# Attention, routed experts and a second MoE on one core: exponentials side by side for the product with V, and ids, gathers, low parts and flags in another order

## The chip, the core and the metric

The kernel runs on one core of a Trainium2 chip. The core has TensorE (PE: matmuls and transposes into PSUM), VectorE (DVE), ScalarE (ACT), GpSimd (POOL) and SyncE (SP, which issues most transfers), each with a queue of its own that it works through in order; the 16 DMA engines move data between HBM and SBUF. The metric is the device time of one launch in microseconds; lower is better.

## What is computed

```python
def _attn_ref(q, k, v, f):                    # B=4, H=8, S=576, D=64
    scores = np.matmul(q, k.transpose(0, 1, 3, 2)) / np.sqrt(D)
    cum = np.cumsum(np.log(np.clip(f, 0.0001, 1.0)), axis=-1)
    scores = scores + cum[:, :, :, None] - cum[:, :, None, :]
    scores = np.where(causal, -1000000000.0, scores)
    attn = np.exp(scores - np.max(scores, axis=-1, keepdims=True))
    attn = attn / (np.sum(attn, axis=-1, keepdims=True) + 1e-09)
    return np.matmul(attn, v)

def _moe_ref(x, modality_id, w_gate, modality_bias, w1, w2):   # N=2304, D=512, E=8, F=1024
    logits = x @ w_gate + modality_bias[modality_id]
    e_idx = np.argmax(logits, axis=1)
    gate_w = softmax(logits)[np.arange(N), e_idx]
    for e in range(E):
        mask = e_idx == e
        out[mask] = gate_w[mask, None] * (np.maximum(x[mask] @ w1[e], 0.0) @ w2[e])

def _moe2_ref(x, w1, w2, w3, w_out):          # d_ff=768
    return np.maximum(np.maximum(x @ w1, x @ w2), x @ w3) @ w_out
```

The rows of the attention's output, 4 x 576 tokens of 512, go through the routed experts and then through the second MoE.

## The kernel before

By the times of its trace the kernel has three stages: attention with the routing and one "early" expert to 303 us, the slots of the other experts to 505, and the second MoE to the end.

**Attention.** The 576 keys and queries of a head are cut into four blocks of 128 and a tail of 64 (index 4; `BLK` holds start and length). Scores stand transposed, keys on the partitions. The tails of four heads share one tile (`tail_scores`, exponentials in `p4`). The rest of a head is three parts of 512 columns (`PARTS`, L436): each lists pieces (key block, query blocks, first column, last column), gets its matmuls (`st_mm`: L424 for the fp16 main part, L426 for a second part of low bits, decay and maximum), one exponential on ScalarE (L461) into `pt`, and a mask of the diagonal blocks on GpSimd (`causal`, L432). "all", "13" and "23" name sets of query blocks in the layout of q, which stores them in the order 0, 2, 1, 3. `WHERE` (L439) says in which part and column the exponentials of a pair of blocks lie.

**The product with V.** `av` (L470) multiplies the exponentials with `vb`, 64 columns of V and a column of ones, in f32. The first four query blocks of a head go to a PSUM tile `avt` of 512 columns (L490), the tail's 64 columns to columns 384 to 448 of one of two accumulators, `accs[h % 2]` (L487), in five products of 64. `av_sb` copies both on ScalarE to `os` (L495 for the tail, L496 for the 512), `av_tr` transposes `os` back into columns 0 to 325 of the same accumulator (L503), and VectorE divides by the sum of the row into `xacc` (L511 to L513).

**The order.** Attention runs in steps, one for each part of each head, 24 a batch; a step is about 2 us in the middle of the attention. `at(step, function, priority)` puts work into a step's agenda (`run_step` works it off), and `later(step, f, n, priority)` runs f in its step and what f returns n steps later. A head's products with V follow its scores by `AVL` = 5 steps. The instructions of an engine then stand in the order in which they were issued. Of the work in the agenda these pieces matter here:
- `second_q` (L1103): at the start, the transposed q of the second four heads of batch 0 is copied from PSUM to `qs` (L257 on VectorE, L255 on ScalarE) and doubled into q's second half (`dup`, L281).
- the maxima: products `m` on PE (L334 to L337), reduced on VectorE (L328).
- `mod_tr` in step 14 and `bias` in step 16 (L1141, L1142): the modality ids of all tokens are converted (`mc`, L987 to L989), transposed on PE (`mt`, L991) and turned into the bias of the logits (L997 to L1005). The logits that the bias is added to are made for the first time at the end of batch 0.
- `plan_early` (L824): the early expert is chosen from the first two batches' routing, its 256 tokens are gathered from DRAM, where `xd` holds the attention's rows as fp16 high and low parts, by two gathers issued by GpSimd (`e_gather`, L778, in steps 84 and 90, `EPL` + 10 and + 16), and transposed by SP into `ev` (L779) three steps later. Its matmuls start at `e_h(0)` (L789).
- `x_cols(0, 6)` in step 97 (L953): of the last batch's rows the columns of six heads are split into a high part on ScalarE and a low part on GpSimd (L544), one instruction for the four blocks of 128 rows and one for the tail.
- after the last step `route` computes ranks with one-hots `oh` (L657) and small products (L663 to L667).

**The slots.** `slot(s)` (L1454) runs expert work for one or two tiles of 128 tokens: `hgroup` (L1411 to L1416) makes the hidden layer, `ytile` the output rows, which GpSimd scatters. `split_next(s, ...)` splits the next slot's weights inside `tc.If(flag)`, where the flag is read on each engine (L1437).

## Time and profile before

| | before |
|---|---|
| median of 3 runs, us | 794.81 (793.76 to 798.06) |
| profiled execution, us | 798.22, its span 796.4 |
| mean granted TensorE clock | 0.969 |
| PE busy, us | 738.0 (93%) |
| VectorE, ScalarE, GpSimd busy, us | 405.9, 287.5, 223.2 |
| matmuls, DMA packets | 5244, 147105 (98.01 MB) |

The profiled execution is at the upper end of the runs. Its span is the time from the first to the last instruction; 1.8 us lie around it. Times within the trace count from the start of the span. "Busy" says when an engine was at work, not whether anybody waited for it. An idle time before an instruction is given in brackets with what ended it.

### The profile page before, as it was taken

The page shows a single profiled execution, that of the slowest core. Times are in us where ns is not written, and L with a number is a line of the kernel's source. Part 1 is how long each engine was busy: PE and PEld are TensorE (multiplying, and loading weights), DVE is VectorE, ACT ScalarE, POOL GpSimd, SP SyncE. Part 2 cuts the span into 40 slices and gives each one's busy share as a digit, 9 for nine tenths or more (in the row PEclk, how much of TensorE's full clock was granted, in tenths as well). Part 3 has the DMA queues.
Part 4 walks back from the last instruction along what each step waited for, and adds up shares of the span by engine and source line. Part 5 has one row for each costly group of instructions (what it writes and reads, how often), then busy time and mean ns, then how long its engine had stood idle before and what let it go on. Part 6 is the DMA issues. An engine that isn't in the chain of part 4 may idle for free.

```text
span 796.4 us, 14004 instructions
## 1 busy us (share of the span) xinstructions
PE 738.0 (93%) x5244; PEld 451.0 (57%) x5244; DVE 405.9 (51%) x862; ACT 287.5 (36%) x494; POOL 223.2 (28%) x374
## 2 busy tenths in 40 slices
PE   6886999999996987899999998799999999999996
PEld 3564667667764755666666665344444444444483
DVE  7775766765773374786984487398011021011010
ACT  7462545553453124433652265144111111111121
POOL 5551254353485010341122111012211211211211
PEclk9898999999998799999999999899999999999998
...
GB/s 168 143 57 187 98 169 199 101 159 55 205 101 80 25 168 306 191 143 340 269 169 133 265 256 202 186 221 1 53 1 1 106 0 1 67 13 1 40 14 27
DMA packets 147105, 98.01 MB, mean 123 GB/s; under 512 B 110576, under 2 KB 127076, under 8 KB 147013
## 3 DMA queue, kind: packets, MB, share of 16 engines
...
q14 instruction: 37, 0.30, 0.1%
...
## 4 chain that ended last, share of the span: by engine, by line
PE 44%; DVE 5%; issue 3%; DMA 2%; ACT 0%; POOL 0%; POOLq 0%; SPq 0%; ACTq 0%; DVEq 0%
PE a L1555 7%; PE a L1556 7%; PE a L1557 7%; PE y L1425 3%; PE o L1581 3%; PE h L1412 3%; PE h L1411 3%; PE y L1424 3%; PE h L1413 3%; PE y L1423 3%; PE o L1580 3%; PE o L1579 3%; DMA x2d<-ysb,ids 2%; DVE dec L1197 1%; DVE dec L1198 1%
## 5 line engine op out<-in xcount | busy, mean ns | idle before, releaser
L1555 PE MATMUL a<-xt,mwh 128*128 128x512 f16 (+1 forms) x360 | 130.0, 361 | 4.5 <-DVEq L1523 4.5
L1556 PE MATMUL a<-xt,mwh 128*128 128x512 f16 (+1 forms) x360 | 130.0, 361 | 0.0
L1557 PE MATMUL a<-xt,mwl 128*128 128x512 f16 (+1 forms) x360 | 129.8, 361 | 0.0
L432 POOL TENSOR_SCALAR_AFFINE_SELECT pt<-pt 64x128 f32<-64x128 f32 (+1 forms) x192 | 73.3, 382 | 98.7 <-ACT pt L461 87.7
L1561 DVE TENSOR_TENSOR s<-a,s 128x512 f32<-128x512 f32 (+1 forms) x30 | 19.1, 637 | 157.9 <-PE a L1557 156.7
L490 PE MATMUL avt<-pt,vb 128*65 128x128 f32 (+2 forms) x384 | 91.4, 363 | 2.7 <-POOL pt L432 2.6
L1411 PE MATMUL h<-xt,wh 128*128 128x256 f16 (+1 forms) x320 | 81.3, 264 | 6.4 <-DMA xt<-xg 4.2
L461 ACT ACTIVATE pt<-t 128x512 f32<-128x512 f32 x96 | 57.1, 596 | 80.5 <-PE t L426 77.4
L1564 POOL TENSOR_TENSOR hl<-s,hh 128x512 f16<-128x512 f32 (+1 forms) x30 | 32.8, 1093 | 186.2 <-ACT hh L1563 186.2
L1412 PE MATMUL h<-xt,wh 128*128 128x256 f16 (+1 forms) x320 | 81.4, 264 | 0.0
L1413 PE MATMUL h<-xt,wl 128*128 128x256 f16 (+1 forms) x320 | 81.3, 264 | 0.0
L328 DVE TENSOR_REDUCE cm<-m 128x1 f32<-128x512 f32 (+4 forms) x136 | 66.7, 533 | 10.2 <-PE m L337 8.0
L1387 DVE SCALAR_TENSOR_TENSOR wl<-raw,wh 128x1024 f16<-128x1024 f32 x48 | 57.0, 1221 | 14.5 <-ACT wh L1386 13.7
...
L1563 ACT ACTIVATE hh<-s 128x512 f16<-128x512 f32 (+1 forms) x30 | 17.6, 587 | 114.5 <-DVE s L1562 114.4
L1555 PEld LDWEIGHTS <-mwh 128*128 128x128 f16 x360 | 35.5, 99 | 40.6 <-DVEq L1523 5.0
L1425 PE MATMUL y<-wh,hl 128*128 128x512 f16 x144 | 54.6, 379 | 2.5 <-DVE hl L1416 2.0
L1557 PEld LDWEIGHTS <-mwl 128*128 128x128 f16 x360 | 35.5, 99 | 35.5 <-issue 1.4
L1556 PEld LDWEIGHTS <-mwh 128*128 128x128 f16 x360 | 35.5, 99 | 35.3 <-issue 1.1
L1423 PE MATMUL y<-wh,hh 128*128 128x512 f16 x144 | 54.6, 379 | 1.0 <-ACT hh L1415 1.0
L1386 ACT ACTIVATE wh<-raw 128x1024 f16<-128x1024 f32 x48 | 48.8, 1050 | 17.9 <-DMA raw<-in_moe_w_dram 10.6
L1424 PE MATMUL y<-wl,hh 128*128 128x512 f16 x144 | 54.6, 379 | 0.0
(328 smaller groups left out, 1407.4 us busy)
## 6 DMA issues: line engine op xcount, KB each, us to landing
...
```

The lines of the kernel that those rows point to most:

```text
L328: nc.vector.tensor_reduce(out=out, in_=in_, axis=AX.X, op=ALU.max)
L432: nc.gpsimd.affine_select(out=o, in_=o, pattern=[[0, nb], [1, 2], [2, HP]], base=-r2, channel_multiplier=-2, compare_op=ALU.is_ge, fill=0.0)
L490: nc.tensor.matmul(o[:D1, o0:o0 + n], vb[:, jb, h, :], pt[:, w, c0:c0 + n], start=(jb == 0), stop=(jb == min(o0 // 128 // 2 + 2 * (o0 // 1 ...
L1411: nc.tensor.matmul(ph[:, k], w1_(WH, s, c, fb), xt[:, c, 0:w], start=(c == 0), stop=False)
L1412: nc.tensor.matmul(ph[:, k], w1_(WH, s, c, fb), xt[:, NC + c, 0:w], start=False, stop=False)
L1413: nc.tensor.matmul(ph[:, k], w1_(WL, s, c, fb), xt[:, c, 0:w], start=False, stop=(c == NC - 1))
L1423: nc.tensor.matmul(py, hh[:, c, rs], w2_(WH, s, c), start=(c == 0), stop=False)
L1424: nc.tensor.matmul(py, hh[:, c, rs], w2_(WL, s, c), start=False, stop=False)
L1425: nc.tensor.matmul(py, hl[:, c, rs], w2_(WH, s, c), start=False, stop=(c == NF - 1))
L1555: nc.tensor.matmul(ps[:, :n], mwh[i][:, c, fs], xt[:, c, :n], start=(c == 0), stop=False)
L1556: nc.tensor.matmul(ps[:, :n], mwh[i][:, c, fs], xt[:, NC + c, :n], start=False, stop=False)
L1557: nc.tensor.matmul(ps[:, :n], mwl[i][:, c, fs], xt[:, c, :n], start=False, stop=(c == NC - 1))
```

## The change

1. Scores: part 0 has its query blocks in natural order ("nat"); part 1 begins with (block 0, tail) and goes on with key block 1 against 1, 2, 3 and the tail; part 2 holds key block 3 against 3 and the tail, then key block 2 against 2, 3 and the tail. So the exponentials of a key block stand side by side, and `av` issues products of 128 (into columns 384 to 512 of the accumulator), 448, 448, 320, 192 and 64 columns for a head. The copies are of 128 and 448 columns, the masks of part 2 pick their two blocks out of 384 columns.
2. `second_q`: all four copies on VectorE, the doubling of each half right behind its two, first in its step.
3. The ids: steps 26 and 27 instead of 14 and 16.
4. Both gathers of the early expert in step 97, their transposes two steps later.
5. `x_cols(0, 6)` two steps later, its low part in four pieces of 128 x 384 and one of 64 x 384.
6. In a slot of one tile the next slot's split, with its flag, stands before the output rows.

```diff
--- before.py
+++ after.py
@@ -296,6 +296,8 @@
         def sub(v_, cs):
             if cs == "all":
                 return v_
+            if cs == "nat":
+                return v_.rearrange("p a (b x) -> p b a x", b=2)
             if cs == "23":
                 return v_[:, :, 128:256]
             if cs == "01":
@@ -426,16 +428,16 @@
                 nc.tensor.matmul(o, part2(r, "k", 97, h, jb), part2(r, "q", 97, h, ib), start=False, stop=True, skip_group_check=True)
 
 
-        def causal(x, nb):
+        def causal(x):
+            nb = x.shape[1]
             for r2 in range(2):
-                o = x[HP * r2:HP * r2 + HP].rearrange("p (b r j) -> p b r j", b=nb, j=HP)
+                o = x[HP * r2:HP * r2 + HP].rearrange("p b (r j) -> p b r j", j=HP)
                 nc.gpsimd.affine_select(out=o, in_=o, pattern=[[0, nb], [1, 2], [2, HP]], base=-r2, channel_multiplier=-2, compare_op=ALU.is_ge, fill=0.0)
 
 
-        PARTS = (((0, "all", 0, 512),),
-                 ((1, "13", 0, 256), (1, 2, 256, 384), (0, 4, 384, 448), (1, 4, 448, 512)),
-                 ((3, 3, 0, 128), (2, "23", 128, 384), (2, 4, 384, 448), (3, 4, 448, 512)))
-        WHERE = {(0, 0): (0, 0), (0, 2): (0, 128), (0, 1): (0, 256), (0, 3): (0, 384), (1, 1): (1, 0), (1, 3): (1, 128), (1, 2): (1, 256), (3, 3): (2, 0), (2, 2): (2, 128), (2, 3): (2, 256), (0, 4): (1, 384), (1, 4): (1, 448), (2, 4): (2, 384), (3, 4): (2, 448)}
+        PARTS = (((0, "nat", 0, 512),),
+                 ((0, 4, 0, 64), (1, 1, 64, 192), (1, "23", 192, 448), (1, 4, 448, 512)),
+                 ((3, 3, 0, 128), (3, 4, 128, 192), (2, "23", 192, 448), (2, 4, 448, 512)))
 
         def tail_scores(u):
             b, hh = divmod(u, 2)
@@ -459,47 +461,40 @@
                 r["pt", h] = pt_p.tile([P, 3, 512], F32, tag="pt", name="pt", bufs=PTB)
             pt = r["pt", h][:, w]
             nc.scalar.activation(out=pt, in_=t, func=AF.Exp, scale=SC)
-            return lambda: causal(pt[:, 0:256] if w == 2 else pt[:, 0:128], 2 if w == 2 else 1)
+            blocks = (pt[:, 0:128], pt[:, 64:192], pt[:, 0:384])[w].rearrange("p (b x) -> p b x", b=1 + w // 2)
+            return lambda: causal(blocks[:, :, 0:128])
 
 
         D1 = D + 1
         TC = 384
 
-        AVP = ((0, ((0, 0, 512, 0),)), (1, ((1, 0, 256, 256), (1, 256, 128, 128))), (2, ((2, 128, 128, 128), (2, 256, 128, 384))), (3, ((2, 0, 128, 384),)))
+        AVP = ((128, 448, 0), (576, 448, 0), (1216, 320, 128), (1024, 192, 256))
 
         def av(b, h, jbs):
             r = bt[b]
-            vb, pt, p4 = r["vb"], r["pt", h], r["tail", h // HU]
+            vb, pt, p4 = r["vb"], r["pt", h].rearrange("p w x -> p (w x)"), r["tail", h // HU]
             if jbs[0] == 0:
                 r["o", h] = ps_w.tile([P, 512], F32, tag="o", name="avt")
+                nc.tensor.matmul(accs[h % 2][:D1, TC:TC + P], vb[:, 0, h, :], pt[:, 0:P], start=True, stop=True)
             o = r["o", h]
-            ot = accs[h % 2][:D1, TC:TC + HP]
             hc = HP * (h % HU)
             for jb in jbs:
                 if jb == 4:
-                    for k_ in range(NB):
-                        rows = HP if k_ == 4 else P
-                        if k_ == 4:
-                            x = p4[:, hc:hc + HP]
-                        else:
-                            w, cc = WHERE[k_, 4]
-                            x = pt[:, w, cc:cc + HP]
-                        nc.tensor.matmul(ot, vb[:rows, k_, h, :], x, start=(k_ == 0), stop=(k_ == 4))
+                    nc.tensor.matmul(o[:D1, 384:448], vb[:HP, 4, h, :], p4[:, hc:hc + HP], start=False, stop=True, skip_group_check=True)
                     continue
-                for w, c0, n, o0 in AVP[jb][1]:
-                    nc.tensor.matmul(o[:D1, o0:o0 + n], vb[:, jb, h, :], pt[:, w, c0:c0 + n], start=(jb == 0), stop=(jb == min(o0 // 128 // 2 + 2 * (o0 // 128 % 2), 9) or jb == 3), skip_group_check=True)
+                c0, n, o0 = AVP[jb]
+                nc.tensor.matmul(o[:D1, o0:o0 + n], vb[:, jb, h, :], pt[:, c0:c0 + n], start=(jb == 0), stop=(jb > 0), skip_group_check=True)
 
         def av_sb(b, h):
             r = bt[b]
             r["os", h] = sm.tile([D1, 512 + HP], F32, tag="os", name="os")
-            nc.scalar.activation(out=r["os", h][:, 512:512 + HP], in_=accs[h % 2][:D1, TC:TC + HP], func=AF.Copy)
-            nc.scalar.activation(out=r["os", h][:, 0:512], in_=r["o", h][:D1, :], func=AF.Copy)
+            nc.scalar.activation(out=r["os", h][:, 0:P], in_=accs[h % 2][:D1, TC:TC + P], func=AF.Copy)
+            nc.scalar.activation(out=r["os", h][:, P:576], in_=r["o", h][:D1, 0:448], func=AF.Copy)
 
         def av_tr(b, h):
             x = bt[b]["os", h]
             for ib in range(NB):
-                n = BLK[ib][1]
-                c = (0, 256, 128, 384, 512)[ib]
+                c, n = BLK[ib]
                 nc.tensor.transpose(accs[h % 2][:n, 65 * ib:65 * ib + 65], x[:, c:c + n], identf[:D1, :D1])
 
         def av_out(b, h):
@@ -541,7 +536,9 @@
             for y, n, cs in ((r["xh", 0], P, slice(0, 4)), (r["xh", 2], HP, slice(4, 5))):
                 xr = r["x"][:n, cs].rearrange("p c h d -> p c (h d)")[:, :, d]
                 nc.scalar.activation(out=y[:, :, 0, d], in_=xr, func=AF.Copy)
-                lo.append(lambda y=y, xr=xr: eng.tensor_tensor(out=y[:, :, 1, d], in0=xr, in1=y[:, :, 0, d], op=ALU.subtract))
+                for c in range(0, cs.stop - cs.start, 1 if hn > 2 else 4):
+                    c_ = slice(c, min(c + (1 if hn > 2 else 4), cs.stop - cs.start))
+                    lo.append(lambda y=y, xr=xr, c_=c_: eng.tensor_tensor(out=y[:, c_, 1, d], in0=xr[:, c_], in1=y[:, c_, 0, d], op=ALU.subtract))
             return lambda: [f_() for f_ in lo]
 
         def x_part(r, nm, c0, cn):
@@ -824,7 +821,7 @@
                 at(g + 4, later(g + 4, f, 1, 5), 6)
             at(g + 3, rows, 6)
             for r in range(2):
-                at(g + 10 + 6 * r, later(g + 10 + 6 * r, lambda r=r: e_gather(r), 3, 9), 8)
+                at(g + 23, later(g + 23, lambda r=r: e_gather(r), 2, 9), 8)
             for c in range(8):
                 s_ = g + ESP[c]
                 at(s_, lambda c=c: e_split(c)[0](), 8)
@@ -950,7 +947,7 @@
                 plan_x(b, 24 * (b + 1) + AVL + 2)
         plan_fin(B - 1)
         plan_early(EPL)
-        gx = 24 * (B - 1) + 3 * 5 + AVL + 5
+        gx = 24 * (B - 1) + 3 * 5 + AVL + 7
         at(gx, later(gx, lambda: x_cols(0, 6, GE_), 1, 5), 6)
         for u in range(1, NU):
             plan_max(u)
@@ -1106,10 +1103,9 @@
             def f():
                 for a in range(2):
                     c_[0](VE, a)
-                    c_[1](SE, a)
-                for a in range(2):
+                    c_[1](VE, a)
                     dup(0, "q", a, HU, HU)
-            at(1, f, 6)
+            at(1, f, 0)
         at(0, second_q, 6)
         def load1():
             new_kq(1)
@@ -1138,8 +1134,8 @@
         at(7, wgs)
 
         at(6, meta, 9)
-        at(14, mod_tr, 6)
-        at(16, bias)
+        at(26, mod_tr, 6)
+        at(27, bias)
         run_step(0)
         e_()()
         for g in range(1, NS_ + AVL + 6):
@@ -1468,9 +1464,12 @@
                 split_next(s, spl[g])
                 if (s, g) in ROWS:
                     ROWS[s, g]()
+            if n == 1:
+                split_next(s, spl[4])
             for r in range(n):
                 ytile(s, r)
-                split_next(s, spl[4 + r])
+                if n > 1:
+                    split_next(s, spl[4 + r])
                 if r == (s == 0):
                     fetch_next(s)
                 if nj:
```

**GpSimd, the end of the attention.** `pt` are exponentials, `exg` the gathered rows, `xh` the split rows of the last batch. Before:

```order
L432 AFFINE_SELECT pt<-pt 64x256 [waits Activation_49]
L432 AFFINE_SELECT pt<-pt 64x256
L778 DMA exg<-xd,xi 128x1024 [waits Pool_49]
L432 AFFINE_SELECT pt<-pt 64x128 [waits Activation_49]
L432 AFFINE_SELECT pt<-pt 64x128 [waits DMASW1_49]
L432 AFFINE_SELECT pt<-pt 64x128 [waits Activation_49]
L432 AFFINE_SELECT pt<-pt 64x128
L432 AFFINE_SELECT pt<-pt 64x256 [waits Activation_49]
L432 AFFINE_SELECT pt<-pt 64x256
```

After:

```order
L435 AFFINE_SELECT pt<-pt 64x128 [waits Activation_49]
L435 AFFINE_SELECT pt<-pt 64x128
L435 AFFINE_SELECT pt<-pt 64x2x128 [waits Activation_49]
L435 AFFINE_SELECT pt<-pt 64x2x128
L775 DMA exg<-xd,xi 128x1024 [waits DVE_49,Pool_49]
L775 DMA exg<-xd,xi 128x1024
L541 TENSOR_TENSOR xh<-xacc,xh 128x384 [waits DMAHW1_49,DMAHW0_49,DMAHW4_49,DVE_49,Activation_49]
L541 TENSOR_TENSOR xh<-xacc,xh 128x384 x3
L541 TENSOR_TENSOR xh_3462<-xacc,xh_3462 64x384 [waits DMAHW1_49,DMAHW0_49,Activation_49]
```

Before, a mask behind the second gather waits for a gather's transfer (DMASW1); afterwards both gathers stand behind the last mask, and the low parts, in five pieces, behind them.

**PE, the products with V of one head** with those of the next scores left out at the breaks. `acc_136` and `acc_137` are the two accumulators. Before, the first product and the later ones:

```order
L503 MATMUL acc_137<-identf,os 64x65
L490 MATMUL avt<-pt,vb 65x512 [waits PE_49,Pool_49]
...
L490 MATMUL avt<-pt,vb 65x256 [waits Pool_49]
L490 MATMUL avt<-pt,vb 65x128
L490 MATMUL avt<-pt,vb 65x128 [waits Pool_49]
L490 MATMUL avt<-pt,vb 65x128
...
L490 MATMUL avt<-pt,vb 65x128
L487 MATMUL acc_136<-pt,vb 65x64 [waits DVE_49]
L487 MATMUL acc_136<-pt,vb 65x64 x3
L487 MATMUL acc_136<-p_542,vb 65x64
```

After, the same head's:

```order
L498 MATMUL acc_137<-identf,os 64x65
L478 MATMUL acc_136<-pt,vb 65x128 [waits DVE_49,Pool_49]
L486 MATMUL avt<-pt,vb 65x448 [waits PE_49]
...
L486 MATMUL avt<-pt,vb 65x448 [waits Pool_49]
L486 MATMUL avt<-pt,vb 65x320 [waits Pool_49]
...
L486 MATMUL avt<-pt,vb 65x192
L483 MATMUL avt<-p_542,vb 65x64
```

There are six products instead of eleven, and the wait for VectorE stands at the first of them instead of the first of 64 columns; the others of the same head stand at other steps, as before.

**VectorE, the modality ids.** `q_1_135<-qs` is the doubling of batch 1's q, `cm` the maxima. Before:

```order
L281 COPY q_1_135<-qs 64x4x512 [waits DMAHW1_49]
L511 TENSOR_SCALAR rs<-acc_136 128x5 [waits PE_49,Activation_49]
L512 RECIPROCAL rs<-rs 128x5 [waits DVE_49]
L987 MEMSET mc 64x64 [waits DMAHW0_49]
L988 CAST mc<-mi 16x64x2 [waits DMAHW2_49,DMAHW7_49,DMAHW0_49,DVE_49]
L989 CAST mc<-mi 4x64 [waits DMAHW3_49]
L281 COPY q_1_135<-qs 64x4x512 [waits DMAHW2_49]
L513 TENSOR_TENSOR xacc<-acc_136,rs 128x5x64
L328 TENSOR_REDUCE cm<-m 128x1 [waits PE_49] x2
L328 TENSOR_REDUCE cm<-m 128x1
L328 TENSOR_REDUCE cm<-m 128x1 [waits PE_49]
L997 CAST mf<-mt 128x4x4
```

After:

```order
L506 TENSOR_SCALAR rs<-acc_136 128x5 [waits PE_49]
L330 TENSOR_REDUCE cm<-m 128x1 x3
L507 RECIPROCAL rs<-rs 128x5 [waits DVE_49]
L984 MEMSET mc 64x64
L985 CAST mc<-mi 16x64x2 [waits DMAHW0_49,DVE_49]
L986 CAST mc<-mi 4x64
L508 TENSOR_TENSOR xacc<-acc_136,rs 128x5x64
L330 TENSOR_REDUCE cm<-m 128x1 [waits PE_49]
L330 TENSOR_REDUCE cm<-m 128x1
L994 CAST mf<-mt 128x4x4 [waits PE_49]
L995 CAST mf<-mt 128x4
L999 TENSOR_SCALAR nm<-mf 128x20 [waits DVE_49]
```

The conversions no longer stand between the two doublings; they come later, behind the reading of another head (`rs`), with the bias three rows further on.

## Rows read from the trace of the kernel before

**Rows 1.** Windows: busy of PE, PEld, DVE, ACT, POOL; PEclk, DMA share, GB/s

```profile
86.00:244.00 158.00, 152.81 (x1557) 110.23 (x1557) 108.52 (x308) 78.79 (x164) 79.22 (x166) 1.00 0.68 135
244.00:303.00 59.00, 44.88 (x333) 32.05 (x333) 29.05 (x100) 13.87 (x23) 14.02 (x18) 0.83 0.35 87
```

**Rows 2.** PE timeline: start, busy us, line, out<-in, count, [idle <-what ended it]

```profile
32.98 0.40 PE L336 MATMUL m<-k,q 67*128 67x512 f16 x1 [1.70 <-DVE q L281]
```

**Rows 3.** VectorE timeline around 30 us

```profile
29.16 0.73 DVE L257 COPY qs<-tpq 128x512 f16<-128x512 f16 x2
...
31.15 1.77 DVE L281 COPY q<-qs 64x1024 f16<-64x1024 f16 x2 [1.26 <-ACT qs L255]
```

**Rows 4.** Windows of low clock, columns as in rows 1

```profile
33.20:40.00 6.80, 6.80 (x43) 4.35 (x42) 4.64 (x10) 1.49 (x3) 6.26 (x15) 0.50 0.18 28
246.50:261.90 15.40, 11.88 (x92) 8.65 (x93) 5.13 (x17) 3.92 (x7) 7.34 (x12) 0.72 0.22 18
```

**Rows 5.** PE timeline: products with V, and the next product

```profile
154.00 0.63 PE L487 MATMUL acc<-pt,vb 128*65 128x64 f32 x8
154.57 0.33 PE L487 MATMUL acc<-p,vb 64*65 64x64 f32 x2
...
237.57 1.02 PE L490 MATMUL avt<-pt,vb 128*65 128x512 f32 x2
238.43 0.60 PE L597 MATMUL xtp<-identf,xacc 128*128 128x128 f32 x4
```

**Rows 6.** PE and VectorE timelines: transposes of a head, reading of the head before

```profile
237.21 0.52 PE L503 MATMUL acc<-identf,os 65*128 65x65 f32 x5 [0.27 <-ACT os L496]
...
233.76 0.49 DVE L513 TENSOR_TENSOR xacc<-acc,rs 128x320 f32<-128x320 f32 x1
```

**Rows 7.** PE and VectorE timelines at the ids; VectorE over 65.30:66.10 and 72.05:73.47

```profile
66.17 0.23 PE L991 MATMUL mt<-ident,mc 64*128 64x64 f16 x1 [4.88 <-DVE mc L989]
...
69.37 0.63 PE L336 MATMUL m<-k,q 67*128 67x512 f16 x1
...
68.60 0.69 DVE L281 COPY q<-qs 64x2048 f16<-64x2048 f16 x1 [2.50 <-DMA qs<-hlq]
...
sum 2.22, DVE 2.05; mean DVE 1.03
```

**Rows 8.** PE timeline, 246 to 267 us

```profile
246.54 1.97 PE L490 MATMUL avt<-pt,vb 128*65 128x512 f32 x2 [2.64 <-POOL pt L432]
...
258.36 0.17 PE L663 MATMUL rank<-oh,tri 128*128 128x8 f16 x1 [2.63 <-DVE oh L657]
...
266.55 0.42 PE L789 MATMUL eh<-ev,ewk 128*128 128x256 f16 x1
```

**Rows 9.** GpSimd timeline, 246 to 260 us, and VectorE's one-hots

```profile
246.19 3.30 POOL L432 TENSOR_SCALAR_AFFINE_SELECT pt<-pt 64x128 f32<-64x128 f32 x9 [3.30 <-DMA exg<-xd,xi]
250.06 0.87 POOL L432 TENSOR_SCALAR_AFFINE_SELECT pt<-pt 64x256 f32<-64x256 f32 x2 [0.57 <-ACT pt L461]
255.16 3.96 POOL L544 TENSOR_TENSOR xh<-xacc,xh 128x1536 f16<-128x1536 f32 x2 [4.23 <-issue]
...
256.01 2.30 DVE L657 TENSOR_TENSOR oh<-r,r 128x40 f16<-128x40 f32 x1
...
275.81 0.20 DVE L657 TENSOR_TENSOR oh<-r,r 128x40 f16<-128x40 f32 x1
```

**Rows 10.** GpSimd and PE timelines: gathers of two slots, products that use them

```profile
292.73 1.97 POOL L1401 DMA_INDIRECT xg<-xd,idg  x1 [17.25 <-DVE vld L1312]
...
301.50 0.94 POOL L1401 DMA_INDIRECT xg<-xd,idg  x1 [4.55 <-DMA xt<-xg]
...
303.31 0.37 PE L1411 MATMUL h<-xt,wh 128*128 128x256 f16 x1 [4.15 <-DMA xt<-xg]
...
328.06 0.27 PE L1411 MATMUL h<-xt,wh 128*128 128x256 f16 x1 [2.28 <-SPq L1442]
```

**Rows 11.** VectorE timeline in a slot with a flag that is false

```profile
495.61 0.42 DVE L1416 SCALAR_TENSOR_TENSOR hl<-h,hh 128x256 f16<-128x256 f32 x1 [0.30 <-DVEq L1437]
```

## The prediction

> **What bounds the kernel now.** I read the table of windows first. In the attention from 86 to 244 us TensorE (PE) is busy for 152.8 of 158.0 us, so there its own time counts; in the passage from attention to the expert slots, 244 to 303, it is busy for 44.9 of 59.0 at a granted clock of 0.83, so there its waits count [rows 1]. Idle time of VectorE, ScalarE or GpSimd costs nothing unless PE waits behind it. So I ask of each edit two things: does it take time from PE where PE sets the pace, or does it take away a wait of PE that nothing else replaces? Then I read PE's timeline for those waits, and the timelines of VectorE and GpSimd for what stands before their ends. Behind some waits the granted clock falls to 0.50, which is 1.2 of 2.4 GHz; such a stretch loses half its length, and this is a second price of the wait.
>
> **The change part by part.** All terms are made against the profiled execution, 798.2 us, which is 3.4 over the median of 794.8; I take the difference over to the median.
>
> *A, the second pair of q copies.* PE stands idle for 1.70 us before 32.98, until VectorE has doubled q [rows 2]. VectorE had made its own two copies, 0.73 from 29.16, then waited 1.26 us for ScalarE's two, then doubled both halves, 1.77 from 31.15 to 32.92 [rows 3]. Afterwards all four copies are its own: 29.16 + 2 x 0.73 + 1.77 = 32.39 against 32.92, **-0.5**. The added copies lie in VectorE's idle time. From 33.2 to 40.0 the granted clock is 0.50 [rows 4]: 6.8 us, of which 3.4 are lost. If a shorter stall let the clock stay, 3.4 more would come back; 1.2 us instead of 1.7 is still a stall, so I don't count on it. Bounds 0 (something else of the start is as late) and -3.9.
>
> *B, the products with V.* Per head the columns stay 1600 (512 + 384 + 256 + 128 + 320 before, 128 + 448 + 448 + 320 + 192 + 64 after). The products go from 11 to 6, each in two f32 passes, so ten passes go. What a pass costs beside its columns: two passes of 512 start at 237.57 and the next product at 238.43, 0.86 us for 1024 columns or 0.84 ns each; eight passes of 64 last from 154.00 to 154.57, 0.57 where 512 x 0.84 would be 0.43 [rows 5]. So the five products of 64 pay some 0.14 us a head for being small, and over the 25 heads or so between 86 and 244 this is 3.4 us, on PE that is busy there 97% of the time [rows 1]. Second, the copies of a head's result: at 237.21 PE has waited 0.27 us for ScalarE's second copy [rows 6], one of ten waits of about that size from 108 to 244. That copy gets 448 columns instead of 512, and the first can start after the first product instead of after the last five; I take 0.18 off each, 1.8. The sum is 5.2, of which I take **-4.5**, since PE will meet some other wait sooner. Bounds: -2 (less than half of it) and -6.3 (0.25 a head). Heads outside that stretch I count at nothing: before 86 transfers and VectorE set the pace, after 244 the waits of D.
>
> The edit also adds a wait: a head's first product now writes the accumulator that VectorE reads for the head two before, and all of PE's next scores are queued behind it. In the trace that reading starts at 233.76 and takes 0.49; the first product stands at 237.57 [rows 5, 6]. The slack is 3.3 us, so it costs nothing.
>
> A rule speaks against B. The Trainium skill, "TensorE: Matmul & The Clock Gate", section "Wait — 56ns, not 53.3ns?", gives a fixed cost of about 2.5 ns to a matmul beside its columns. By it ten passes less would bring, as an estimate, 10 x 2.5 ns x 25 = 0.6 us instead of 3.4. The row disagrees: a pass of 64 columns takes 71 ns where its columns' share is 54. I go by the row; the rule's outcome is close to the second rival.
>
> *C, the modality ids, twelve steps later.* At 66.17 PE has waited 4.88 us for VectorE's conversion of the ids, which stood behind a doubling of q that waited for a transfer. It looks like the prize of the change. But PE's next maxima, at 69.37, need the second doubling, which starts at 68.60 after 2.50 us of waiting for its own transfer and takes 0.69, to 69.29 [rows 7]. Without the ids PE does the 3.2 us of work between sooner and waits for the same 69.29. The wait moves, the end doesn't: 0. At the new place VectorE gets the conversions and the bias arithmetic, together 2.1 us [rows 7], and PE a transpose that waits for the former. VectorE is 69% busy in that stretch [rows 1], so a part may make the next maxima late: **+0.5**, with bounds +2.1 (all of it shows) and -1.3 (the arithmetic leaves a place where it made PE late and is covered at the new one).
>
> *D, the gathers and the low parts at the end of the attention.* At 246.54 PE has waited 2.64 us for a causal mask [rows 8], because GpSimd waited 3.30 for a gather to land that it had issued ahead of the mask [rows 9]. Afterwards both gathers stand behind the last mask, and no mask waits for a transfer: 2.6. At 258.36 PE has waited 2.63 for VectorE's one-hot [rows 8]; this comparison of 40 columns took 2.30 us at 256.01, while GpSimd made two low parts (3.96 from 255.16), and 0.20 at 275.81 with GpSimd quiet [rows 9]. Afterwards the low parts are five pieces, two steps later: 2.1. Behind these stalls the granted clock over 246.5 to 261.9 is 0.72 [rows 4]: 15.4 x 0.28 = 4.3 us, which I take as saved when there is no stall of that size. Together **-9.0**: the early expert's first product, at 266.55 [rows 8], would come at 257.6.
>
> What can be late next is that product's own input. The last masks, at 250.06 and 0.87 long [rows 9], move up by the first stall and a part of the clock's loss and end at about 247.2; from there the gathers go. From a first gather's issue to the product that uses it there are two rows: 292.73 to 303.31, 10.6 us, in the first slot, and 301.50 to 328.06, 26.6, in the second [rows 10]. The former is nearer (two gathers and two transposes one after the other, nothing else in flight that they need) and gives 257.8: just in time. On SP the two transposes move behind the last rows of batch 2, and behind them stand only writes that wait for the low parts; GpSimd's low parts stand behind the gathers, and only those writes wait for them. Bounds of D: -9.6 (all of the second stall) and -2.6 (the first stall alone, no clock). The last heads, routing and the slots hang on this chain and shift with it.
>
> The slow one-hot agrees with a rule: the Trainium skill, "SBUF — State Buffer", section "Who interferes with whom", lets a VectorE instruction with two SBUF inputs contend with a GpSimd one that reads SBUF, the later waiting for the whole of the other. If the one-hot still meets one of the five pieces it would by that rule lose, as an estimate, up to a fifth of 3.96, 0.8 us.
>
> *E, the flag read ahead of a single slot's rows.* A flag that is false costs VectorE 0.30 us between two instructions [rows 11], in either place; the rows of two slots are written a little later and no PE work waits for them. 0, bounds -0.3 and +0.3.
>
> Sum: -0.5 - 4.5 + 0.5 - 9.0 + 0 = -13.5. The profiled execution would come to 784.7, the median to **781.3 us**.
>
> **The rivals.** *First, the slower side: the late gather is late.* If it takes what the second slot's took, the product comes at 247.2 + 26.6 = 273.8 instead of 257.6: +16.2, 797.5. It decides from 24 us between issue and use (slower than before), 28 for more than half a per cent. For it: both gathers leave at once, at the last moment. Against it: the DMA share in this stage is 0.35 [rows 1], and PE has the last heads to do. *Second, only columns count:* B gives 0, 785.8. For it: passes follow each other without a gap; against it: the rows of 64 columns. *Third, the clock stays up at 33 us:* 781.3 - 3.4 = 777.9. *Fourth, the 4.88 us at 66 do come out,* with half of the low clock behind them, 2.2: 774.2; the doubling that ends at 69.29 speaks against it. *Fifth, the new wait of a head's first product:* it decides from 3.3 us of delay of VectorE's reading; 0.8 us at each of 25 heads would be +20, 801.3. The slack speaks against it.
>
> **How the numbers follow.** Half a per cent, about 4 us, is what a measurement of this kernel can tell from no change. Chances: the forecast .53 (.03 of it within half a per cent, where D and B both fall to their bounds), only columns .18, the clock at 33 us .16, the ids .03, the late gather .06 (half within, half slower), the new wait .04. Faster .50 + .18 + .16 + .03 = .87, same .03 + .03 = .06, slower .03 + .04 = .07. The range: downward the third rival with B's bound is 776, and with part of C's 774; upward D's bound alone is 787.7, with a part of the second rival 789. Half of the ids' case, the late gather, the new wait and the forecast's tails are left out, some .18: **774 to 789**.
>
> **What would show it.** No mask that waits for a transfer and no stall of PE at 246; the one-hot at 0.2 to 1.0 us; the early expert's first product 13 us earlier than 266.55, of which 9 arise behind 244; a granted clock above 0.83 in that passage. Between 86 and 244 the same steps in about 4.5 us less. At 66 a wait of PE for q in the place of that for the ids. At 33 a wait of about 1.2. The prediction is wrong if the early expert's first product waits long for its transposed input, if a head's first product waits for VectorE, or if the attention before 244 is no shorter.

## The result, and the profile after

| | before | after |
|---|---|---|
| median, us (14 runs each) | 797.06 | 788.11 |
| lowest to highest, us | 792.57 to 801.78 | 784.19 to 794.25 |
| ratio, 95% interval | | 0.9876 (0.9855 to 0.9897) |
| profiled execution's span, us | 796.4 | 786.9 |
| mean granted TensorE clock in it | 0.969 | 0.98 |
| PE busy, us | 738.0 | 730.9 |
| matmuls | 5244 | 4924 |

The change makes the kernel faster by 1.2%: 9.0 us by the medians, 9.9 by the ratio. The forecast was 13.5 us, and 781.3 us in a range from 774 to 789; 788.1 lies in the range, near its upper end. Of the 6.8 us between 781.3 and 788.1, 2.3 come from the starting point, since three runs of the kernel before had a median of 794.81 and 14 runs have 797.06. One run below, of 798.10 us, counted as slow and is left out of the time and the ratio of its kernel ("after, first product late").

Windows of the trace of after come first, columns as in [rows 1]: the stretch and its length, busy time (count) of PE, PEld, DVE, ACT and POOL, then PEclk, DMA share and GB/s.

```profile
86.00:244.00 158.00, 153.95 (x1342) 93.22 (x1340) 111.10 (x324) 80.57 (x168) 82.04 (x175) 1.00 0.67 133
244.00:303.00 59.00, 48.64 (x384) 34.73 (x383) 31.13 (x100) 19.83 (x29) 13.86 (x13) 0.94 0.61 179
...
33.20:40.00 6.80, 6.21 (x60) 4.09 (x59) 6.04 (x14) 2.61 (x5) 6.26 (x14) 1.00 0.16 25
237.60:253.90 16.30, 15.27 (x137) 10.49 (x135) 5.81 (x26) 7.00 (x15) 10.71 (x17) 0.98 0.50 98
```

In the passage behind 244 us the granted clock rose from 0.83 to 0.94, and at 33 us it is 1.00 here where [rows 4] has 0.50. Stretches cut at fixed times compare different work, though. So I cut both traces at the same work instead: VectorE's reading of a head (heads counted from 0 over the batches), the early expert's first product, the first product of slots 0 and 1, the second MoE's first product, the end of the span. Each column is the time from the cut before it to its own, in us:

| kernel | start to head 11 | head 11 to 28 | head 28 to early expert | to slot 0 | to slot 1 | to second MoE | to the end |
|---|---|---|---|---|---|---|---|
| before | 133.2 | 107.0 | 26.5 | 36.8 | 24.8 | 177.1 | 291.2 |
| after | 133.5 | 104.1 | 16.3 | 34.4 | 26.6 | 179.1 | 292.9 |
| difference | +0.4 | -2.9 | -10.2 | -2.4 | +1.9 | +2.0 | +1.7 |

The sum is -9.5, the difference of the spans. The second and third column are where B (the products with V) and D (the gathers and low parts at the end of the attention) were expected. What is given back in the last three must be read with the experiments' rows, below: the last column runs over code that no kernel here changes.

PE's timeline of after, the waits that answer to [rows 2, 7, 8] (start, busy, form, and in brackets the idle time ahead with what ended it):

```profile
32.31 0.39 PE L338 MATMUL m<-k,q 67*128 67x512 f16 x1 [0.90 <-DVE q L281]
...
60.51 0.66 PE L478 MATMUL acc<-pt,vb 128*65 128x128 f32 x2 [3.46 <-DVE xacc L508]
67.14 0.39 PE L338 MATMUL m<-k,q 67*128 67x512 f16 x1 [0.75 <-DVE q L281]
...
101.18 0.20 PE L988 MATMUL mt<-ident,mc 64*128 64x64 f16 x1 [1.98 <-DVE mc L986]
...
247.71 0.17 PE L660 MATMUL rank<-oh,tri 128*128 128x8 f16 x1 [0.49 <-DVE oh L654]
...
253.90 0.42 PE L786 MATMUL eh<-ev,ewk 128*128 128x256 f16 x1
```

VectorE's timeline there, for [rows 3]:

```profile
29.30 0.73 DVE L257 COPY qs<-tpq 128x512 f16<-128x512 f16 x2
30.07 0.42 DVE L281 COPY q<-qs 64x1024 f16<-64x1024 f16 x1
30.41 0.74 DVE L257 COPY qs<-tpq 128x512 f16<-128x512 f16 x2
31.19 1.07 DVE L281 COPY q<-qs 64x1024 f16<-64x1024 f16 x1
```

VectorE no longer waits for ScalarE there, and PE's stall at 33 has shrunk from 1.70 to 0.90; the two of 2.6 behind 244 are gone or down to 0.49; the early expert begins without a wait, 12.65 us sooner than the 266.55 of [rows 8]. Two waits are new: 3.46 at 60.5, of a head's first product for VectorE's reading, and 1.98 at 101, of the ids at their new place. GpSimd and VectorE at the end of the attention, to be read against [rows 9]:

```profile
242.91 0.88 POOL L435 TENSOR_SCALAR_AFFINE_SELECT pt<-pt 64x256 f32<-64x256 f32 x2 [1.47 <-ACT pt L463]
244.08 1.18 POOL L775 DMA_INDIRECT exg<-xd,xi  x1 [0.30 <-DVE r L650]
245.56 0.95 POOL L775 DMA_INDIRECT exg<-xd,xi  x1 [0.30 <-issue]
249.10 4.38 POOL L541 TENSOR_TENSOR xh<-xacc,xh 128x384 f16<-128x384 f32 x5 [2.59 <-ACT xh L538]
...
247.49 0.16 DVE L654 TENSOR_TENSOR oh<-r,r 128x40 f16<-128x40 f32 x1
```

No mask waits for a transfer. The one-hot takes 0.16 us, since the low parts begin 1.6 us behind it.

### The profile page after: what moved, and what is told of

The parts are those of the page before. It is cut to its first block, busy times and chain, and to the rows that moved or that the text cites. A ratio compares the mean times of both kernels' runs of the same rounds, so it can differ in the third digit from the quotient of the medians.

```text
span 786.9 us, 13335 instructions
## 1 busy us (share of the span) xinstructions
PE 730.9 (93%) x4924; PEld 421.9 (54%) x4924; DVE 403.8 (51%) x864; ACT 286.5 (36%) x492; POOL 227.5 (29%) x377
## 5 line engine op out<-in xcount | busy, mean ns | idle before, releaser
L435 POOL TENSOR_SCALAR_AFFINE_SELECT pt<-pt 64x128 f32<-64x128 f32 (+1 forms) x192 | 76.9, 400 | 95.4 <-ACT pt L463 89.1
L1560 DVE TENSOR_TENSOR s<-a,s 128x512 f32<-128x512 f32 (+1 forms) x30 | 19.1, 637 | 157.9 <-PE a L1556 156.7
L486 PE MATMUL avt<-pt,vb 128*65 128x448 f32 (+2 forms) x256 | 95.6, 478 | 0.0
L1562 ACT ACTIVATE hh<-s 128x512 f16<-128x512 f32 (+1 forms) x30 | 17.6, 587 | 114.5 <-DVE s L1561 114.4
```

The source lines that it names most:

```text
L435: nc.gpsimd.affine_select(out=o, in_=o, pattern=[[0, nb], [1, 2], [2, HP]], base=-r2, channel_multiplier=-2, compare_op=ALU.is_ge, fill=0.0)
L486: nc.tensor.matmul(o[:D1, o0:o0 + n], vb[:, jb, h, :], pt[:, c0:c0 + n], start=(jb == 0), stop=(jb > 0), skip_group_check=True)
```

## The experiments

Each kernel differs from before or from after by one piece. The letters are the prediction's: A for the q copies, B for the products with V, C for the ids, D for the gathers and low parts, E for the flag. First what they measured, cut as above, with the ratio to the kernel before that ran beside them:

| kernel | ratio (95% interval) | start to head 11 | 11 to 28 | 28 to early expert | to slot 0 | to slot 1 | to second MoE | to the end |
|---|---|---|---|---|---|---|---|---|
| after without E | 0.9884 (0.983 to 0.9939) | 135.4 | 104.6 | 16.2 | 34.6 | 25.7 | 179.0 | 291.4 |
| after without C | 0.9914 (0.9884 to 0.9944) | 136.2 | 103.9 | 16.2 | 34.8 | 25.8 | 177.8 | 294.7 |
| after without D | 1.0002 (0.9984 to 1.002) | 132.1 | 104.0 | 26.0 | 35.1 | 25.5 | 177.5 | 292.3 |
| after without B | 0.9934 (0.9903 to 0.9964) | 136.5 | 106.5 | 17.6 | 35.9 | 24.8 | 177.2 | 293.9 |
| before, gathers | 0.9944 (0.9908 to 0.9979) | 135.7 | 107.0 | 19.4 | 34.3 | 25.2 | 178.6 | 291.8 |
| before, low parts | 0.9939 (0.9914 to 0.9965) | 134.7 | 107.0 | 21.7 | 34.6 | 24.8 | 177.6 | 291.2 |
| after, gathers later | 0.9971 (0.9949 to 0.9992) | 130.6 | 104.7 | 24.4 | 34.9 | 25.9 | 176.4 | 292.4 |
| before, B alone | 0.9991 (0.9958 to 1.0024) | 134.0 | 104.0 | 27.9 | 34.6 | 25.8 | 180.2 | 291.6 |
| after, first product late | 0.9847 (0.9806 to 0.9887) | 135.8 | 104.1 | 16.4 | 34.8 | 24.9 | 181.5 | 292.5 |
| after without A | 0.9869 (0.9842 to 0.9897) | 136.0 | 104.3 | 16.3 | 34.9 | 26.8 | 177.8 | 292.0 |
| before, D alone | 0.9906 (0.9873 to 0.9938) | 135.3 | 107.1 | 16.8 | 34.8 | 25.7 | 177.0 | 291.0 |
| after, ids converted ahead | 0.989 (0.9852 to 0.9929) | 137.1 | 104.1 | 16.3 | 34.7 | 25.9 | 180.4 | 292.4 |

The column "11 to 28" repeats to 0.8 us among kernels that have the same edits (103.9 to 104.7 with B, 106.5 to 107.1 without). So does "28 to early expert" where D is in, with the gathers in their place (16.2 to 16.4 with B, 16.8 and 17.6 without). Where PE's stalls stay it doesn't: "after without D" and "before, B alone" are the same there and took 26.0 and 27.9. The first column and the last three spread too: the same instructions take 291.0 to 294.7 at the end, and the start took 130.6 to 135.4 in four kernels that are the same there (after, without E, without D, gathers later). A difference of 2 us in those columns of a single trace is therefore no finding, and the +1.9, +2.0 and +1.7 above are none.

**The tail of the attention (D).** Undone:

```diff
-                at(g + 23, later(g + 23, lambda r=r: e_gather(r), 2, 9), 8)
+                at(g + 10 + 6 * r, later(g + 10 + 6 * r, lambda r=r: e_gather(r), 3, 9), 8)
...
-        gx = 24 * (B - 1) + 3 * 5 + AVL + 7
+        gx = 24 * (B - 1) + 3 * 5 + AVL + 5
...
-                for c in range(0, cs.stop - cs.start, 1 if hn > 2 else 4):
-                    c_ = slice(c, min(c + (1 if hn > 2 else 4), cs.stop - cs.start))
-                    lo.append(lambda y=y, xr=xr, c_=c_: eng.tensor_tensor(out=y[:, c_, 1, d], in0=xr[:, c_], in1=y[:, c_, 0, d], op=ALU.subtract))
+                lo.append(lambda y=y, xr=xr: eng.tensor_tensor(out=y[:, :, 1, d], in0=xr, in1=y[:, :, 0, d], op=ALU.subtract))
```

> The changed kernel with the gathers of the early expert and the low parts of the last batch where they were (edit D undone, all else changed). Theory: D is worth 9 to 10 us: PE's stalls of 2.6 us each at a mask near 244 and at a one-hot near 255 are back with the low clock behind them, the early expert's first product is at 263 to 264 instead of 253.9, total 797 to 798, the time of the kernel before or above. Rival (the two stalls alone count, the clock has other causes): first product at 258 to 259, total 792 to 793.

Measured: 798.97 us, 1.0002, the time of the kernel before. So as long as D is missing, the other four edits together bring nothing that the times show. The granted clock hides some of it: over the runs, the span times its mean clock (an estimate of the time at full clock) is 771.3 us against 773.4 in the 15 runs of the kernel before beside it, 2 us less, while low clock takes 24.9 us instead of 22.2. PE's timeline of this kernel has both stalls again, as the theory said, and the passage from head 28 took 26.0 us; the first product came at 262.04, a little before the forecast of 263.

```profile
242.59 0.69 PE L478 MATMUL acc<-pt,vb 128*65 128x128 f32 x2 [3.11 <-POOL pt L435]
...
254.43 0.17 PE L658 MATMUL rank<-oh,tri 128*128 128x8 f16 x1 [2.58 <-DVE oh L652]
```

Then the same edit the other way round, in the kernel before: the gathers alone (the first line of the diff above, reversed), the low parts alone (the rest), and both.

> The kernel before with one edit: both gathers of the early expert in step 97 and their transposes two steps later. Theory: this takes away the wait of the mask (2.6 us at 246) and the low clock behind that stall (2.5), and leaves the one-hot's stall of 2.6 behind the two large low parts with the low clock behind it; from the reading of head 28 to the early expert's first product it takes some 21.5 us instead of 26.4 before and 16.3 in the changed kernel; total 5 us under the kernel before. Rival: the clock is one thing for both stalls and only returns when both are gone; then 24 us there and 2.6 in total.

> The kernel before with one edit: the last batch's low parts two steps later and in five pieces. Theory: the one-hot takes 0.2 to 1.0 us instead of 2.3 and PE's stall of 2.6 before it shrinks to 0.5, with the clock back to full behind it; the mask's stall of 2.6 at 246 stays with its low clock. From the reading of head 28 to the early expert's first product some 22.6 us instead of 26.4; total 4 us under the kernel before. Rival: the one-hot's slowness has another cause than GpSimd's low part and it takes 2.3 us again: no change.

> The kernel before with gathers and low parts both as in the changed kernel (edit D alone). Theory: the parts add up less than fully, since both stalls feed one stretch of low clock: each alone gave 3.5 to 5 us; together 8 to 9, with 17 to 18 us from the reading of head 28 to the early expert's first product (26.4 before), total 789 to 790. Rival: the parts add up or more, total 788, as fast as the changed kernel, and the other edits are worth nothing together.

The gathers alone: 794.78 us, 0.9944, the passage 19.4 instead of the 21.5 expected. The low parts alone: 793.17, 0.9939, 21.7 instead of 22.6. Both: 790.45, 0.9906, 16.8. PE's timeline with the gathers alone has only the second stall, with the low parts alone only the first:

```profile
255.48 0.17 PE L663 MATMUL rank<-oh,tri 128*128 128x8 f16 x1 [2.58 <-DVE oh L657]
```

```profile
248.04 1.10 PE L490 MATMUL avt<-pt,vb 128*65 128x512 f32 x2 [2.59 <-POOL pt L432]
...
256.88 0.17 PE L665 MATMUL rank<-oh,tri 128*128 128x8 f16 x1 [0.49 <-DVE oh L659]
```

So each stall has the cause that was read from the trace. The one-hot's goes because the low parts now begin behind it (258.33 behind 256.66 with the low parts alone); their cutting into five pieces is tested by no run, since no piece meets the one-hot.

In the passage of these single traces the two edits are worth 7.1 and 4.8 us alone and 9.6 together, less than their sum. Windows of the passage before, with the gathers alone, and with the low parts alone (columns as in [rows 1]):

```profile
240.10:266.55 26.45, 20.03 (x168) 15.75 (x167) 7.94 (x27) 7.23 (x15) 10.10 (x16) 0.78 0.34 58
```

```profile
242.67:262.02 19.35, 15.64 (x168) 13.02 (x166) 7.95 (x27) 7.23 (x15) 10.60 (x15) 0.98 0.36 86
```

```profile
241.66:263.33 21.67, 17.44 (x167) 14.08 (x166) 6.14 (x27) 7.21 (x15) 10.54 (x19) 0.90 0.43 71
```

The length times one minus the granted clock is an estimate of what low clock takes: 5.8 us before, 0.4 with the gathers alone, 2.2 with the low parts alone, nothing with both (clock 1.00). The rest is 20.6, 19.0, 19.5 and 16.8 us. So at full clock the parts bring 1.7 and 1.1 alone and 3.8 together; it is the low clock that they share, with 5.4 and 3.7 alone and 5.8 together. These are single traces: over the runs the mean spans are shorter by 4.3, 4.4 and 7.6 us, too close to a plain sum for the intervals to tell. D alone is a ratio of 0.9906, 7.5 us of the kernel's 9.9.

**The late gather, the slower rival made real.** In after:

```diff
-                at(g + 23, later(g + 23, lambda r=r: e_gather(r), 2, 9), 8)
+                at(g + 27, later(g + 27, lambda r=r: e_gather(r), 2, 9), 8)
```

> The changed kernel with both gathers and their transposes four more steps later (step 101). This is the slower rival of the prediction made real. Theory: the gathers then stand behind the low parts on GpSimd and are issued near 254 instead of 244 us; from issue to use it takes about 10 us as in the changed kernel (244.1 to 253.9), so the early expert's first product waits for its transposed input and comes at 263 to 265, and the total is about 10 us over the changed kernel, 798, no gain left. Rival: other work covers the wait, total 788 to 791.

Measured 795.41, 0.9971 against 0.9876: 7.6 us lost of the 9.9, where 10 were expected. GpSimd's and PE's timelines of this kernel:

```profile
246.96 4.38 POOL L541 TENSOR_TENSOR xh<-xacc,xh 128x384 f16<-128x384 f32 x5 [5.37 <-issue]
251.52 1.18 POOL L775 DMA_INDIRECT exg<-xd,xi  x1 [0.18 <-issue]
...
259.70 0.39 PE L786 MATMUL eh<-ev,ewk 128*128 128x256 f16 x1 [6.87 <-DMA ev<-exg]
```

Here the product does wait for its input, so the time from issue to use is measured without a cover: 251.52 to 259.70, 8.2 us. In after the gathers go at 244.08 and the product stands at 253.90; by this its input would be there at 252.3. Counted from the end of SP's issue of the two transposes (257.84 in this kernel, 251.04 in after) it would be there at 252.9. So, as an estimate, 1.0 to 1.6 us are left over. The rival's mechanism is real, and the change stays clear of it by less than two microseconds.

**The products with V (B).** Undone in after, and alone in before (the first hunks of the diff above the prediction, one way or the other; the core of it):

```diff
-        AVP = ((128, 448, 0), (576, 448, 0), (1216, 320, 128), (1024, 192, 256))
+        AVP = ((0, ((0, 0, 512, 0),)), (1, ((1, 0, 256, 256), (1, 256, 128, 128))), (2, ((2, 128, 128, 128), (2, 256, 128, 384))), (3, ((2, 0, 128, 384),)))
```

> The changed kernel with the old layout of exponentials and the eleven products with V (edit B undone). Theory (a pass costs beyond its columns, and the copies are shorter): from the reading of head 9 (118.3 in the changed kernel, 116.9 before) to that of head 28 it takes 123.2 us as in the kernel before, instead of 119.3; total 792. Rival (only columns count): 119.5 us there, total 788. A second rival: the first product's wait for VectorE, 3.46 us at 60.5 in the changed kernel, costs as much as B gains; then this kernel is earlier at 86 us by 1 us or more.

> The kernel before with one edit: the new layout of the exponentials and the six products with V. Theory (0.15 us a head, 17 heads from head 11 to head 28 in 104.2 us instead of 107.0): 3.5 to 4.5 us under the kernel before, 793.5. Rival: the first product's new wait for VectorE takes it back before 86 us, and head 4 is read 1 us or more later than in the kernel before: no change in total.

From head 11 to head 28 it takes 106.5 us in the first, 104.0 in the second: 2.4 to 2.9 us belong to B wherever it stands, 0.14 to 0.17 a head. By the cut that the first theory names, from head 9, it is 121.8 us, between its 123.2 and the rival's 119.5. The totals don't follow as simply. Undone, the time is 792.6 us, 0.9934 against 0.9876. Alone it brings nothing, 798.38 us, 0.9991 (0.9958 to 1.0024). Its rival had said so, but for a cause that is false: head 4 is read at 87.05 us, not later than the 87.30 of before. In the passage behind head 28, which takes 27.9 us instead of 26.5, PE reaches the mask sooner and waits 2.99 us for the same gather instead of 2.64:

```profile
244.45 0.69 PE L478 MATMUL acc<-pt,vb 128*65 128x128 f32 x2 [2.99 <-POOL pt L435]
```

The rest of the 27.9 is granted clock. The kernel "after without D" has the same instructions and stalls there (3.11 and 2.58 us). Windows of the passage in that kernel, then with B alone:

```profile
236.07:262.04 25.97, 19.74 (x136) 11.99 (x135) 7.70 (x26) 7.08 (x15) 10.12 (x16) 0.80 0.27 59
```

```profile
238.05:265.94 27.89, 21.78 (x137) 14.75 (x136) 7.91 (x27) 7.08 (x15) 10.12 (x16) 0.74 0.25 55
```

Low clock takes 5.2 us of the first and 7.2 of the second; before, it was 5.8. What remains is 20.6 to 20.8 in all three. So with the stalls in place B brings nothing in this passage, and the 1.4 us that it seems to lose are a difference in clock between two executions. Over the runs the clock was lower too: its mean is 0.9680 with B alone and 0.9709 in the 28 runs of the kernel before beside it. Span by clock, 796.6 x 0.9680 = 771.1 against 796.5 x 0.9709 = 773.3: at full clock the kernel would be 2.2 us shorter, and 25.5 us go to low clock instead of 23.2. Why the clock was lower there isn't settled; single traces show low stretches at different places from run to run.

What the 2.9 us are is seen in two windows over this stretch, and in PE's waits in it. Windows of before, then of after:

```profile
133.15:240.10 106.95, 103.71 (x1075) 74.80 (x1075) 74.81 (x225) 51.78 (x109) 54.51 (x112) 1.00 0.59 127
```

```profile
133.52:237.61 104.09, 102.48 (x909) 62.40 (x908) 74.70 (x226) 52.01 (x109) 56.01 (x114) 1.00 0.61 128
```

Waits of before, then of after (what waited, for what: us in total, times, longest):

```profile
PE acc L503 <- ACT os L496: 2.4, 9, 0.3
PE m L336 <- DVE cm L328: 0.9, 1, 0.9
```

```profile
PE m L338 <- DVE cm L330: 0.7, 1, 0.7
PE m L338 <- DVE cs L418: 0.2, 1, 0.2
PE acc L498 <- ACT os L492: 0.2, 1, 0.2
```

PE is busy for 1.23 us less, 0.07 a head, and idle for 1.63 less, because the nine waits for the copies, 2.4 us, have shrunk to one of 0.2; shorter gaps, which the lists leave out, take some of that back.

**The new wait of a head's first product.** In after the 128-column product is issued with the last one again, two steps later:

```diff
-                nc.tensor.matmul(accs[h % 2][:D1, TC:TC + P], vb[:, 0, h, :], pt[:, 0:P], start=True, stop=True)
...
                 if jb == 4:
+                    nc.tensor.matmul(accs[h % 2][:D1, TC:TC + P], vb[:, 0, h, :], pt[:, 0:P], start=True, stop=True)
```

> The changed kernel with the 128-column product of a head (into the accumulator) issued two steps later, ahead of the last product of 64 columns, where the wait for VectorE stood before the change. It tests what the new wait costs, 3.46 us at 60.5. Theory: the wait is only a stand-in; the maxima at 67 need a doubling of q that ends at the same time, so PE's wait moves there (3 to 4 us before them), head 4 is read within 1.5 us of the changed kernel, and the total is 787 to 789. Rival: the wait costs its whole length and a stretch of low clock; then 783 to 785.

Measured 787.35, 0.9847 (0.9806 to 0.9887), not to be told from after. PE's timeline has one wait in the place of two, longer than the 3 to 4 us expected, but the maxima behind it start only 1.5 us later, and head 4 is read 0.6 later:

```profile
68.66 0.61 PE L338 MATMUL m<-k,q 67*128 67x512 f16 x1 [7.40 <-DVE q L281]
```

So the wait for the reading was a stand-in. The maxima need the doubling of q, and VectorE's timeline in after shows why it ends when it does: it stands idle for transfers ahead of each doubling.

```profile
59.28 0.69 DVE L279 COPY k<-ks 64x2048 f16<-64x2048 f16 x1 [3.29 <-DMA ks<-hlk]
59.88 0.47 DVE L508 TENSOR_TENSOR xacc<-acc,rs 128x320 f32<-128x320 f32 x1
62.60 0.69 DVE L281 COPY q<-qs 64x2048 f16<-64x2048 f16 x1 [2.24 <-DMA qs<-hlq]
...
66.39 0.69 DVE L281 COPY q<-qs 64x2048 f16<-64x2048 f16 x1 [2.80 <-DMA qs<-hlq]
```

**The ids (C).** Back in steps 14 and 16:

```diff
-        at(26, mod_tr, 6)
-        at(27, bias)
+        at(14, mod_tr, 6)
+        at(16, bias)
```

> The changed kernel with the modality ids back in steps 14 and 16 (edit C undone). Theory: the move costs 1 to 2 us, the wait only changed its place. So PE waits 4 to 5 us for the conversion near 65 us, the next maxima are no later than in the changed kernel by more than 0.5 us, the wait of 1.98 near 101 is gone, the eighth head of batch 0 (106.5 in the changed kernel) is read 1 to 2 us earlier, total 786.5. Rival: the 4.88 us really came out by the move; then everything behind 66 us is 3 to 5 us later and the total is 791 to 793.

Measured 791.07, 0.9914 against 0.9876, with intervals that overlap. The wait for the ids is back, but it is 1.89 us and not 4 to 5, as the reading of a head took 2.16 of it first; the maxima behind it start at 66.56, no later than the 67.14 of after:

```profile
60.29 0.40 PE L478 MATMUL acc<-pt,vb 128*65 128x128 f32 x2 [2.16 <-DVE xacc L508]
63.79 0.20 PE L988 MATMUL mt<-ident,mc 64*128 64x64 f16 x1 [1.89 <-DVE mc L986]
66.56 0.39 PE L338 MATMUL m<-k,q 67*128 67x512 f16 x1 [0.70 <-DVE q L281]
```

So the rival (4.88 us come out at 66) is false: without the move nothing is later at 67. The time 3 us above after was against the theory too, which had 786.5. Behind these waits, up to 118 us, the theory holds: head 9 is read at 115.49 instead of 118.27. Then a product of scores, the first that needs a row of q whose transfer ScalarE issues (`q<-cs`), waits for that transfer:

```profile
119.84 0.28 PE L428 MATMUL t<-q,k 97*64 97x64 f16 x4 [2.32 <-DMA q<-cs]
```

Over the 10 us behind it the granted clock is 0.66, in after 1.00; that is 3.4 us. This wait goes with the place of the ids. From the reading of head 5 to the arrival of PE at this product it takes 27.5 us in after and 25.3 here. In the seven kernels with the ids in step 26, converted there, it is 27.5 to 29.5 (the longer ones at a clock of 0.94), and PE then waits 0.25 us at most; in the other seven it is 25.3 to 26.1 (28.6 with B alone, where another wait of 1.59 stands), and PE waits 0.40 to 2.35. From its issue to its use the transfer takes 4.8 to 6.5 us in these and at most 4.6 in the former; why, no run shows. So the new place costs 2 us there, as the theory had it, and without this cost a wait and, in two traces, low clock take its place. The second of the two converts the ids ahead of their transposition:

```diff
+        at(24, mod_cast, 6)
         at(26, mod_tr, 6)
```

> The changed kernel with the three conversions of the ids on VectorE two steps ahead of their transposition on PE (step 24 instead of 26; the transposition and the bias stay). Theory: at the new place the ids cost PE the 1.98 us of its wait near 101, because the conversion stands behind the maxima on VectorE; two steps ahead VectorE is idle (2.4 us before 96.3 in the changed kernel), so the wait goes, from the reading of head 5 to that of head 8 it takes 17.5 to 18.5 us instead of 19.4, and the total is 786 to 787. Rival: PE's next products wait for the same maxima on VectorE anyway; 19.4 us and 788 again.

Measured 790.0, 0.989. The wait of 1.98 near 101 is down to 0.45. From the reading of head 5 to that of head 8 it takes 20.0 us, where after has 19.4, as the rival had it; but PE reaches the product near 120 after 26.1 us instead of 27.5, so 1.4 are gained. They are lost again in the same wait and in the clock behind it, 0.66:

```profile
120.73 0.28 PE L428 MATMUL t<-q,k 97*64 97x64 f16 x4 [2.35 <-DMA q<-cs]
```

The net worth of C stays open: the medians of these two kernels lie 2 and 3 us above after, which the wait and the low clock of their traces would explain, but the intervals overlap, and C alone in the kernel before was not run.

**The q copies (A) and the flag (E).** Each undone in after by itself. First A:

```diff
-                    c_[1](VE, a)
+                    c_[1](SE, a)
+                for a in range(2):
                     dup(0, "q", a, HU, HU)
-            at(1, f, 0)
+            at(1, f, 6)
```

> The changed kernel with the second pair of q copies on ScalarE again (edit A undone). Theory: PE's stall near 33 is 1.7 us again instead of 0.9, and the granted clock falls behind it to 0.50 for 3 to 8 us, as in the four traces with the old copies; total 2 to 3 us over the changed kernel, 790.5. Rival, the prediction's term without the clock: 0.5 us, 788.6, with the low stretch at 33 as often there as not.

Measured 788.97, 0.9869: not to be told from after, so nearer to the rival's 0.5 than to 2.5, which the intervals don't exclude. The stall at 33 is 1.70 again, as forecast. Of the low clock behind it: the six traces with the old copies all have it. Of eight traces with the new ones two have none (after among them), two a shorter stretch and four one as long as before.

Then E:

```diff
-            if n == 1:
-                split_next(s, spl[4])
             for r in range(n):
                 ytile(s, r)
-                if n > 1:
-                    split_next(s, spl[4 + r])
+                split_next(s, spl[4 + r])
```

> The changed kernel with the flag of a single slot read behind its output rows again (edit E undone). Theory: E costs about 1 us, because in the changed kernel PE waits 1.51 us for the flag before the first product of the second single slot, which it did not before, and gains only 0.6 at the end of the slots. So the wait of 1.51 is gone, from the last y product of the first single slot's predecessor to the second MoE's first product it takes 17.6 us again instead of 18.6, and the time is some 787, 1 us under the changed kernel. Rival, the prediction's term (0): no difference within 0.3 us between these points.

Measured 787.72, 0.9884: no difference in the time. PE's timeline, of after and then of this kernel, from the second single slot to the second MoE:

```profile
479.45 0.23 PE L1407 MATMUL h<-xt,wh 128*128 128x128 f16 x1 [1.51 <-SPq L1438]
...
494.05 0.61 PE L1554 MATMUL a<-xt,mwh 128*128 128x512 f16 x1 [3.88 <-DVEq L1522]
```

```profile
480.16 0.23 PE L1407 MATMUL h<-xt,wh 128*128 128x128 f16 x1 [1.57 <-SPq L1438]
...
495.50 0.61 PE L1551 MATMUL a<-xt,mwh 128*128 128x512 f16 x1 [4.62 <-DVEq L1519]
```

The wait for the flag is there without E as well, so the theory that E brought it is false. What E does is at the end: from the slot's first product to the second MoE it takes 14.6 us with it and 15.3 without, and the wait there is 3.88 against 4.62 (before, the wait was 4.46). All 14 traces agree on this wait: 3.65 to 4.19 with E, 4.46 to 4.88 without. E is a gain of some 0.7 us, too small for the times.

## Why the prediction was right, and where its sizes were off

**D, -9.0.** Right in cause, and in size as far as the trace goes. The passage lost 10.2 us in after, 9.6 with D alone; both stalls and their low clock are gone. The term had 2.6 + 2.1 at the stalls and 4.3 of low clock; D alone gave 3.8 and 5.8, so that the parts were each off and their sum was near. Over the runs D alone was 7.5 us, with an interval from some 5 to 10. Its bound "the first stall alone, no clock" (-2.6) was timid: the gathers alone gave 7.1 in the passage and 4.5 by the ratio. The five pieces, to which the term gave a share of the 2.1, stood behind the one-hot and were not put to the test. The early expert's first product was forecast 13 us earlier and came 12.65 earlier; its input was called just in time at 10.6 us from issue, and has an estimated 1.0 to 1.6 us in hand because the way takes some 8.2.

**B, -4.5.** Mis-sized. The step that failed is "0.14 us a head for being small, over 25 heads". PE's busy time fell by 0.07 a head, half of it. This is shown over 17 heads, from head 11 on, where it makes 1.2 us. For the heads between 86 and 133 us nothing came out: PE was busy there too (45.75 of 47.30 us before), but the wait for the ids, 1.98, stands in that stretch now. So the products' part is 1.2 us instead of 3.4. The rule that was weighed against it (the Trainium skill, "TensorE: Matmul & The Clock Gate", section "Wait — 56ns, not 53.3ns?", 2.5 ns beside a matmul's columns) would give, as an estimate, 10 x 2.5 ns = 0.025 a head; the measured 0.07 lies between it and the row. The error was to read one run of products of 64 columns as the price of all of them; why that run cost more isn't shown. The copies were sized right: 1.8 forecast, 1.6 of idle time gone.

**C, +0.5.** "The wait moves, the end doesn't" was shown: the wait at 66 went to a head's first product (3.46) and from there, in one experiment, to the maxima (7.40), and the maxima always waited for the doubling. The cost at the new place was seen too: 1.98 us of wait, some 2 us up to the product near 120, at the upper bound of the term and not at its +0.5. The term did not look for what stands behind: a transfer for which PE waits when it comes sooner, 0.71 us before and nothing in after. The net isn't known, and may have the other sign.

**A, -0.5.** Right. VectorE's second doubling was forecast to end at 32.39 and ends at 31.19 + 1.07 = 32.26; PE's wait is 0.90 where 1.2 was expected. The rival "the clock stays up at 33 us" came true in after's trace, and wholly in two of eight, against none of six with the old copies. So it is a matter of chance and not a yes or no; that the shorter stall makes it likelier is not shown by so few.

**E, 0.** Mis-sized: 0.7 us of gain, outside its bounds of 0.3. I had looked at the false flag between two slots and not at the last slot, where the second MoE's first product waits for VectorE's flag and finds it read sooner.

**The rivals.** "Only columns count" was nearer to the truth of the products than their term, and wrong on the copies. The new wait of a head's first product exists, at one place, where the slack of 3.3 us read at 233 doesn't hold: VectorE's reading is queued there behind a doubling that waits for a transfer. I had taken the slack from a place in the middle; it cost nothing only because another wait stood behind it.

The sum was 13.5 and the effect 9 to 10. Some 2 us of the difference are B, with 2.4 to 2.9 shown of 4.5. The rest isn't told apart from the spread of the start and of the slots, nor from that of the clock. That the time lies in the range although the effect was a quarter to a third smaller than forecast is owed to the width of the range.
